# Moving the clamps of three weight blocks and the copies of five to GpSimd in a fused attention and feed-forward kernel

## The chip, the cores and the metric

The kernel runs on one core of a Trainium2 chip. Times are device microseconds of that core for one launch, from inputs in the chip's memory to the output in it. A profile is one execution of its own, with its own time; the times shown beside it are other executions.

## The reference

Three parts follow each other; the sizes are batch 4, 8 heads, 576 positions, head width 64, so 512 features.

```python
def _attn_ref(q, k, v):
    ...
    mask = (rel >= 0) & (rel < window)          # window 128
    scores = np.where(mask, scores + bias[None], -1000000000.0)
    attn = np.exp(scores - max)
    attn = attn / (np.sum(attn, axis=-1, keepdims=True) + 1e-09)
    return np.matmul(attn, v)

def _moe_ref(x, U, V, w_ch1, w_ch2):
    h = x.transpose(0, 2, 1) @ U @ V            # rank 32
    u = x + h.transpose(0, 2, 1)
    return u + np.maximum(u @ w_ch1, 0.0) @ w_ch2   # 2048 hidden

def _moe2_ref(x, w_in, w_spatial, b_spatial, w_out):
    h = np.maximum(x @ w_in, 0.0)
    u, v = h[..., :512], h[..., 512:]
    ...                                         # v normalised, mixed over positions
    return (u * v_s) @ w_out
```

The weights U, V, w_ch1, w_ch2, w_in and w_out arrive as 64-bit floats; the rest as 32-bit ones.

## The kernel before

**The work.** The kernel goes through the four batches of the attention, four pairs of heads each (`heads`, from L545). For a pair TensorE makes the scores (L577), VectorE adds the bias and finds the row's extreme (L589), ScalarE takes the exponentials with their sums (L594), and the rows are divided by their sums: L599 and L601 make the reciprocals on VectorE, then nine multiplies a pair follow, each either on GpSimd (L607) or on VectorE (L609). TensorE transposes the result (L616), ScalarE or VectorE copies it out of PSUM (L317, L318), and TensorE multiplies it with the values (L639). After the four pairs of a batch come the transposes of its output (L659) and the low-rank mix (L675, L687), whose result VectorE adds to `u` (L692).

The feed-forward part runs over groups of columns (positions of a batch). Its 2048 hidden units are cut into four parts of four blocks of 128. The **first part** is worked on while the attention still runs: five groups of 256 columns (`ffn_group` with `early`, called at L721) take TensorE's time wherever the attention leaves it, with the lowest priority. Such a group splits `u` into a high and a low half (L431 on ScalarE, L434 on GpSimd), multiplies with the first weights (L460 to L462), takes the positive part (L467, L469), multiplies with the second weights (L497 to L499) and adds (L507). Every float32 product is made as three products of rounded halves: high by high, low by high, high by low. The other columns and parts follow after the attention, then the last network.

**The weights of the first part.** They are eight blocks of 128 x 512, numbered c = 0 to 7: even numbers are the first weights of the four hidden blocks, odd ones the second weights (`part_of_hidden`, L388; called at L710). Each is made by `weights` (L373) in these steps:

- a DMA brings the 64-bit block (512 KB) into a buffer of the ring `wa` (L350);
- ScalarE takes the magnitude of the upper words into a buffer `st` (L356; the ring `st` has three buffers);
- VectorE clamps it to the range of exponents (L362), shifts it and masks it (L363), puts in the sign (L366) and the bits of the lower words (L369), all in place in `st`;
- ScalarE copies `st`, rounded, into the high half (L317, as a CAST that writes `wa`);
- GpSimd subtracts the high half from `st` and writes the low half (L384).

`single` (from L338) has the steps up to L369, and has two forms of the clamp: on VectorE, or on GpSimd if its last argument is true. `weights` has two forms of the high half: the copy on ScalarE, or a multiply by a broadcast 1.0 on GpSimd.

**What sets the order.** All operations are first listed as tasks with an engine (or several to choose from), a cost, what they read and write, and a priority. `Plan.run` (L169) then puts them in order with these costs: at each moment the engine that can begin first takes its ready task of the best priority, and each engine's instructions are written out in that order. It holds one more resource, `port`: a task of GpSimd and a VectorE task marked `port=True` (L362 to L369 and L609 among them) are never planned side by side. The planner's costs for 512 columns are 0.33 for a clamp on VectorE, 0.0034 x 512 + 0.15 = 1.89 for one on GpSimd, 0.52 for a copy on ScalarE and 0.0021 x 512 + 0.15 = 1.23 for an operation of two inputs on GpSimd. On the chip the order of each engine is fixed, and only the semaphore waits decide when an instruction begins. The DMAs are all issued by SyncE, in the planned order.

The constants stand in `K` (L956). `cp` and `wp` are read in one place alone, L712, where they say for each block c of the first part whether its clamp and its copy go to GpSimd:

```python
lambda c: (c < K["cp"], c < K["wp"])
```

Of the kernel before, what the change touches and what calls it, by code (L numbers as in the profile page):

```python
# [259 lines left out]
def tile_kernel(ctx, tc, qT, kT, v, U, V, w1, w2, w_in, wspT, bsp, w_out, bias, out):  # L260
# [32 lines left out]

    r_wa = Ring(in_left, "wa", max(12, 2 * K["parts"][0]))
    r_u = Ring(in_left, "u", 16)
    r_y = Ring(in_left, "y", 12)
    r_raw = Ring(in_left, "raw", 2)
    r_st = Ring(in_left, "st", K["nst"])
    r_h = Ring(in_left, "h", 8)
# [11 lines left out]

    PARTS = K["parts"]

# [10 lines left out]
    def engines(kind, usual):  # L324
        return BOTH if kind in K["flex"] else (usual,)

# [61 lines left out]
    def part_of_hidden(qi, ring, prio, early=lambda c: None, on_pool=lambda c: (False, False)):  # L388
        res = []
        for f in range(PARTS[qi]):  # L390
            c0 = (sum(PARTS[:qi]) + f) * 128
            two = []
            for i, args in enumerate(((block(w1, 0, E, c0, c0 + 128, 4), 4, 128), (block(w2, c0, c0 + 128, 0, E), 1, E))):
                c = 2 * f + i
                two.append(weights(ring, *args, prio(c), early(c), on_pool(c)))
            res.append(two)
        return res
# [142 lines left out]
    def low_rank_weights(prio, early, prio_v, early_v):  # L540
        single(u32, [(0, block(U, 0, 128, 0, RANK)), (1, block(U, 64, S, 0, RANK, 4))], 5, RANK, prio, None, early)
        P.add("DVE", 0.1, lambda: nc.vector.memset(u32[64:, 0], 0.0), w=[u32], prio=prio)
        single(v32, [(0, stacked(block(V, 0, RANK, 0, S), 4))], 1, S, prio_v, None, early_v)
# [152 lines left out]
    for pair in range(4):  # L696
        P.dma(128, 192, lambda pair=pair: nc.sync.dma_start(out=bias_t[:, pair], in_=bias[:, pair]),
              w=[bias_t.part(pair)], prio=20 * pair + 0.5)
    low_rank_weights(15, 2, 10 * K["low"], 10 * K["lowd"])
    parts_w = [None] * 4  # L700
    for b in range(B):
# [7 lines left out]
        if b == 0:  # L709
            parts_w[0] = part_of_hidden(0, r_wa, lambda c: 10 * (K["w0"] + K["w0s"] * c),  # L710
                                        lambda c: 10 * (K["d0"] + K["d0s"] * c),
# [241 lines left out]

K = dict(parts=(4, 4, 4, 4), flex='xeht', cp=0, wp=0, low=6, w0=8, w0s=1.23, nb=5, evac=40.0, nst=3, d0=7, d0s=0.91, lowd=5)  # L956


# [38 lines left out]
```

## Time and profile before

| | us |
|---|---|
| median of 3 runs | 779.35 |
| the three runs | 779.55, 779.35, 773.35 |
| the profiled execution | 775.38 |
| its span, first to last instruction | 773.6 |
| mean granted clock of TensorE, of full speed | 0.990 |

The span is the time from the first to the last instruction of the profiled execution; 1.8 us of its time lie around it. Engines are named in the rows as PE (TensorE's matmuls), PEld (its weight loads), DVE (VectorE), ACT (ScalarE), POOL (GpSimd) and SP (SyncE); L and a number is a line of the kernel. Start times are us from the start of the span.

### The profile page before, as it was taken

Reading aid. Unit: us, or ns where it says so; the run is one execution under the profiler, and the core shown is the slowest. Engines: PE = TensorE matmul, PEld = TensorE weight load, DVE = VectorE, ACT = ScalarE, POOL = GpSimd, SP = SyncE. Lnnn points to the kernel's source line nnn. Section 1 sums busy time; section 2 is a strip of 40 time slices with the busy share of each in tenths; the row PEclk is TensorE's granted clock in tenths of the full one; section 3 lists DMA queues with packets and bytes.
Section 4 is the critical chain, followed back from the end, with each engine's and each line's share of the span. In section 5 each row is a group of like instructions: output and inputs, shape, how many; then the busy total and the mean of one; then the engine's idle time right before and its main releaser. Section 6 shows DMA issues by size and latency. Waiting matters only on the chain.

```text
span 773.6 us, 13053 instructions
## 1 busy us (share of the span) xinstructions
PE 748.1 (97%) x4988; PEld 635.7 (82%) x4988; DVE 414.4 (54%) x1077; ACT 317.7 (41%) x856; POOL 263.7 (34%) x344
## 2 busy tenths in 40 slices
PE   6788999999899999999999999999999999999998
PEld 5566878889677888898888888888898898898987
DVE  5989677576699832237952272222845325325120
ACT  6767566574445422124531242321552332332322
POOL 1253231110655642125861253530555043043021
PEclk9989999999999999999999999999999999999999
DMA  7846213120605100024000110001300100200102
GB/s 216 278 153 187 63 42 114 35 76 1 219 15 175 43 1 1 1 83 134 1 1 0 60 51 1 0 1 50 105 1 1 55 1 1 69 1 1 55 1 68
DMA packets 28834, 45.70 MB, mean 59 GB/s; under 512 B 4964, under 2 KB 18020, under 8 KB 28772
## 3 DMA queue, kind: packets, MB, share of 16 engines
q1 hardware_dynamic: 28772, 44.87, 18.3%
q8 instruction: 39, 0.64, 0.3%
q14 instruction: 23, 0.19, 0.1%
HBM read 40.14 MB, written 4.72 MB: 58 GB/s over the span
## 4 chain that ended last, share of the span: by engine, by line
PE 87%; DVE 9%; ACT 2%; issue 1%; DMA 1%; SPq 0%; POOL 0%; ACTq 0%; DVEq 0%; POOLq 0%
PE sc L497 5%; PE sc L498 5%; PE sc L499 5%; PE at L460 5%; PE at L461 5%; PE at L462 5%; PE at L616 4%; PE at L639 3%; PE acc L497 3%; PE acc L499 3%; PE acc L498 3%; PE f L460 3%; PE at L780 3%; PE at L779 3%; PE at L781 3%; PE f L461 3%
## 5 line engine op out<-in xcount | busy, mean ns | idle before, releaser
L434 POOL TENSOR_TENSOR x<-u,xc 128x64 fp32r<-128x64 f32 (+5 forms) x108 | 92.8, 893 | 134.3 <-ACT xc L431 133.0
L469 DVE SCALAR_TENSOR_TENSOR h<-at,h 128x512 fp32r<-128x512 f32 (+1 forms) x51 | 32.7, 641 | 96.5 <-ACT h L467 96.5
L467 ACT ACTIVATE h<-at 128x512 fp32r<-128x512 f32 (+1 forms) x51 | 28.6, 560 | 125.9 <-PE at L462 125.8
L594 ACT ACTIVATE p<-p,nmax 128x192 f32<-128x192 f32 (+1 forms) x144 | 61.4, 430 | 9.4 <-DVE nmax L589 9.3
L616 PE MATMUL at<-ident,p 128*128 128x128 f32 x272 | 41.6, 296 | 6.2 <-DVE p L609 5.0
L589 DVE CUSTOM_DVE_ANT_0 p<-sc,bias 128x192 f32<-128x192 f32 (+1 forms) x144 | 39.8, 326 | 14.0 <-PE sc L577 13.9
L460 PE MATMUL at<-xc,wb 128*128 128x512 f32 (+1 forms) x120 | 44.2, 368 | 0.0
L497 PE MATMUL sc<-h,wb 128*128 128x512 f32 (+1 forms) x120 | 44.2, 368 | 0.0
L499 PE MATMUL sc<-h,wb 128*128 128x512 f32 (+1 forms) x120 | 44.1, 368 | 0.0
L498 PE MATMUL sc<-h,wb 128*128 128x512 f32 (+1 forms) x120 | 44.1, 368 | 0.0
L462 PE MATMUL at<-x,wb 128*128 128x512 f32 (+1 forms) x120 | 44.1, 368 | 0.0
L461 PE MATMUL at<-xc,wb 128*128 128x512 f32 (+1 forms) x120 | 44.1, 368 | 0.0
L577 PE MATMUL sc<-kr,qr 64*64 64x192 f32 (+2 forms) x576 | 33.5, 332 | 10.7 <-DMA kr<-in_kT 6.7
L616 PEld LDWEIGHTS at<-ident,p 128*128 128x128 f32 x272 | 33.0, 150 | 12.7 <-issue 4.2
L384 POOL TENSOR_TENSOR wa<-st,wa 128x512 fp32r<-128x512 f32 x24 | 32.6, 1367 | 31.4 <-ACT wa L317 27.8
L794 POOL TENSOR_TENSOR u<-y,u 128x576 fp32r<-128x576 f32 x16 | 23.1, 1459 | 55.6 <-ACT u L792 55.6
L384 POOL TENSOR_TENSOR wb<-st,wb 128x512 fp32r<-128x512 f32 x20 | 30.9, 1555 | 31.3 <-ACT wb L317 31.3
L469 DVE SCALAR_TENSOR_TENSOR h<-f,h 128x512 fp32r<-128x512 f32 (+1 forms) x27 | 17.8, 658 | 43.0 <-ACT h L467 42.9
L431 ACT CAST xc<-u 128x64 fp32r<-128x64 f32 (+5 forms) x108 | 38.3, 437 | 3.8 <-PE at L687 3.8
L467 ACT ACTIVATE h<-f 128x512 fp32r<-128x512 f32 (+1 forms) x27 | 15.4, 571 | 53.2 <-PE f L462 52.1
L497 PE MATMUL acc<-h,wa 128*128 128x256 f32 (+1 forms) x108 | 35.6, 329 | 1.5 <-DVE y L507 1.2
L577 PEld LDWEIGHTS sc<-kr,qr 64*64 64x64 f32 x576 | 21.8, 141 | 17.5 <-issue 10.1
(323 smaller groups left out, 2279.2 us busy)
## 6 DMA issues: line engine op xcount, KB each, us to landing
wa<-in_w SPq DMA_DIRECT2D x16, 512.0 KB, 4.9
wb<-in_w SPq DMA_DIRECT2D x16, 512.0 KB, 5.6
qr<-in_qT SPq DMA_DIRECT2D x16, 288.0 KB, 2.9
kr<-in_kT SPq DMA_DIRECT2D x16, 288.0 KB, 3.8
vr<-in_v SPq DMA_DIRECT2D x16, 256.0 KB, 2.8
wa<-in_w_in SPq DMA_DIRECT2D x8, 512.0 KB, 3.5
out<-h SPq DMA_DIRECT2D x15, 256.0 KB, 2.0
wb<-in_w_out SPq DMA_DIRECT2D x4, 512.0 KB, 4.0
```

Source lines behind the costliest of these rows:

```text
L384: P.add("POOL", pool_tt(k * c), lambda: nc.gpsimd.tensor_tensor(out=b[:, 1], in0=st.ap(), in1=f32(b[:, 0]), op=ALU.subtract), r=[st, b.par ...
L434: nc.gpsimd.tensor_tensor(out=tl[il][:, o : o + m], in0=ub[:, s : s + m], in1=f32(th[ih][:, o : o + m]), op=ALU.subtract)
L460: nc.tensor.matmul(o, wt[:, 0, k], a[ia], start=k == 0, stop=False)
L461: nc.tensor.matmul(o, wt[:, 1, k], a[ia], start=False, stop=False)
L462: nc.tensor.matmul(o, wt[:, 0, k], l[il], start=False, stop=k == 3)
L469: P.add("DVE", dve(per * n), lambda f1=f1, hh=hh, hl=hl: nc.vector.scalar_tensor_tensor(out=hl.ap(), in0=f1.ap(), scalar=0.0, in1=f32(hh.a ...
L497: nc.tensor.matmul(o, wt[:, 0, 0, c], hh[:, j], start=i == 0 and x == 0, stop=False, skip_group_check=True)
L498: nc.tensor.matmul(o, wt[:, 1, 0, c], hh[:, j], start=False, stop=False, skip_group_check=True)
L499: nc.tensor.matmul(o, wt[:, 0, 0, c], hl[:, j], start=False, stop=i == len(wts) - 1, skip_group_check=True)
L577: nc.tensor.matmul(s[o : o + 64, c0 : c0 + k1 - k0], qr[d, 64 * t : 64 * t + 64], kr[d, k0:k1], start=True, stop=True, skip_group_check=True)
L594: nc.scalar.activation(out=o(), in_=o(), func=AF.Exp, scale=-1.0, bias=nmax[:, sl, t : t + 1], accum_out=sums[:, sl, t : t + 1])
L616: P.add("PE", 0.109, lambda pt=pt, t=t, half=half, blk=blk: nc.tensor.transpose(pt[:, blk * 128 : blk * 128 + 128], p[:, t, half * 128 : h ...
```

## The change

Two constants change: `cp` from 0 to 3 and `wp` from 0 to 5. With that the clamp of the blocks c = 0, 1, 2 is an instruction of GpSimd instead of VectorE, and the high half of the blocks c = 0 to 4 is made by GpSimd's multiply by one instead of ScalarE's copy. The priorities and the DMAs' due times stay. The order is planned anew with the other engines and costs, so other instructions may change their places, and of the divisions of the softmax rows others may fall to GpSimd or VectorE.

```diff
-K = dict(parts=(4, 4, 4, 4), flex='xeht', cp=0, wp=0, low=6, w0=8, w0s=1.23, nb=5, evac=40.0, nst=3, d0=7, d0s=0.91, lowd=5)
+K = dict(parts=(4, 4, 4, 4), flex='xeht', cp=3, wp=5, low=6, w0=8, w0s=1.23, nb=5, evac=40.0, nst=3, d0=7, d0s=0.91, lowd=5)
```

What these constants choose between, in `single` and in `weights`:

```python
if pool:
    P.add("POOL", 0.0034 * n + 0.15, lambda: nc.gpsimd.tensor_scalar(out=st.ap(), in0=st.ap(), **cut), w=[st], prio=prio)
else:
    P.add("DVE", dve2(n), lambda: nc.vector.tensor_scalar(out=st.ap(), in0=st.ap(), **cut), w=[st], port=True, prio=prio)
...
if on_pool[1]:
    P.add("POOL", pool_tt(k * c), lambda: nc.gpsimd.tensor_tensor(
        out=b[:, 0], in0=st.ap(), in1=one[:, :1].rearrange("p (a b) -> p a b", a=1).broadcast_to([128, k, c]),
        op=ALU.mult), r=[st, one], w=[b.part(0)], prio=prio)
else:
    copy(engines("w", "ACT"), k * c, lambda: b[:, 0], st.ap, None, r=[st], w=[b.part(0)], prio=prio)
```

## Rows read from the trace of the kernel before

**Rows 1.** The page, part 1: busy time, share of span, instructions of each engine.
```profile
PE 748.1 (97%) x4988; PEld 635.7 (82%) x4988; DVE 414.4 (54%) x1077; ACT 317.7 (41%) x856; POOL 263.7 (34%) x344
```

**Rows 2.** Busy time by stretch; after the engines: granted clock, DMA share, GB/s.
```profile
28.00:78.00 50.00, 40.99 (x449) 32.34 (x450) 47.55 (x168) 37.55 (x124) 18.49 (x24) 0.90 0.62 194
20.00:40.00 20.00, 16.50 (x155) 12.41 (x157) 18.57 (x71) 15.04 (x51) 3.75 (x8) 0.88 0.87 285
40.00:60.00 20.00, 16.48 (x192) 12.35 (x192) 18.79 (x60) 14.37 (x47) 12.38 (x16) 0.86 0.43 133
60.00:80.00 20.00, 17.69 (x207) 14.36 (x208) 20.00 (x81) 15.95 (x55) 4.54 (x7) 1.00 0.60 176
80.00:200.00 120.00, 119.56 (x1349) 102.05 (x1348) 79.92 (x316) 67.54 (x236) 19.76 (x45) 1.00 0.18 53
200.00:220.00 20.00, 16.05 (x84) 13.36 (x83) 16.89 (x30) 10.65 (x22) 15.28 (x16) 1.00 0.63 225
34.00:36.00 2.00, 0.44 (x2) 0.47 (x3) 2.00 (x9) 1.41 (x3) 0.40 (x1) 0.80 0.75 205
36.00:38.00 2.00, 1.72 (x9) 1.32 (x8) 2.00 (x6) 1.07 (x2) 0.97 (x1) 0.50 0.96 311
```

Each row begins with the stretch and its length; then come the busy times (with instructions) of PE, PEld, DVE, ACT and POOL.

**Rows 3.** Timeline of TensorE: start, duration, instruction; in brackets the idle time before.
```profile
35.56 1.30 PE L616 MATMUL at<-ident,p 128*128 128x128 f32 x5 [2.57 <-DVE p L609]
...
52.03 0.41 PE L460 MATMUL f<-x,wa 128*128 128x256 f32 x1
...
66.86 1.70 PE L616 MATMUL at<-ident,p 128*128 128x128 f32 x13 [0.62 <-DVE p L609]
...
73.44 0.36 PE L460 MATMUL f<-x,wa 128*128 128x256 f32 x1
```

**Rows 4.** Groups by line of VectorE, 28 to 78: count, busy us, mean ns, idle.
```profile
L609 DVE TENSOR_SCALAR p<-p,rinv 128x192 f32<-128x192 f32 (+2 forms) x24 | 9.1, 444 | 0.0
L369 DVE SCALAR_TENSOR_TENSOR st<-wa,st 128x512 uint32<-128x512 uint32 x7 | 5.4, 777 | 0.0
L366 DVE SCALAR_TENSOR_TENSOR st<-wa,st 128x512 uint32<-128x512 uint32 x7 | 5.1, 729 | 0.0
...
L363 DVE TENSOR_SCALAR st<-st 128x512 uint32<-128x512 uint32 x8 | 3.9, 484 | 0.0
L362 DVE TENSOR_SCALAR st<-st 128x512 f32<-128x512 f32 x8 | 3.8, 473 | 0.0
```

**Rows 5.** Timeline of VectorE.
```profile
24.70 2.06 DVE L609 TENSOR_SCALAR p<-p,rinv 128x64 f32<-128x64 f32 x9
...
34.85 0.40 DVE L362 TENSOR_SCALAR st<-st 128x512 f32<-128x512 f32 x1
35.17 3.06 DVE L609 TENSOR_SCALAR p<-p,rinv 128x64 f32<-128x64 f32 x9
...
64.98 3.19 DVE L609 TENSOR_SCALAR p<-p,rinv 128x64 f32<-128x64 f32 x9
```

A row of several instructions in a run, as x9, names the shape of its first.

**Rows 6.** ScalarE: one group by line, 28 to 78, then two rows of its timeline.
```profile
L317 ACT CAST wa<-st 128x512 fp32r<-128x512 f32 x7 | 4.3, 615 | 2.4 <-DVE st L369 2.2
...
34.90 0.62 ACT L317 CAST wa<-st 128x512 fp32r<-128x512 f32 x1
36.69 0.48 ACT L317 COPY ph<-at 128x384 f32<-128x384 f32 x1 [1.17 <-PE at L616]
```

**Rows 7.** GpSimd: the subtraction to 100 us (ns least/median/most), the select from the groups.
```profile
L384 POOL TENSOR_TENSOR wa<-st,wa x8: 1262/1286/1371, 35.6 to 84.8; 128x512 fp32r<-128x512 f32 x8
...
masks.py:199 POOL TENSOR_SCALAR_AFFINE_SELECT ident<-ident 128x128 f32<-128x128 f32 x1 | 0.3, 292 | 0.0
```

**Rows 8.** Timeline of GpSimd.
```profile
35.60 1.37 POOL L384 TENSOR_TENSOR wa<-st,wa 128x512 fp32r<-128x512 f32 x1 [3.81 <-ACT wa L317]
...
57.16 1.69 POOL L607 TENSOR_TENSOR p<-p,rinv 128x64 f32<-128x64 f32 x4 [1.28 <-DVE nmax L589]
58.81 1.26 POOL L384 TENSOR_TENSOR wa<-st,wa 128x512 fp32r<-128x512 f32 x1
65.23 1.32 POOL L384 TENSOR_TENSOR wa<-st,wa 128x512 fp32r<-128x512 f32 x1 [5.16 <-ACT wa L317]
```

## The prediction

> **What bounds the kernel now.** I read the busy shares of the page first, to see which engine can set the end: TensorE is busy for 748.1 us of a span of 773.6, 97% [rows 1]. So nearly all of the time is matmul work that this change leaves alone, and what it can win or lose is TensorE's idle time. The second view is the table of stretches, which shows where that idle time lies [rows 2]: 3.50 us in 20 to 40, 3.52 in 40 to 60, 2.31 in 60 to 80, then 0.44 in the whole of 80 to 200, and 3.95 in 200 to 220. From 80 on TensorE has filler (hidden-layer groups of batches already done), so a delay that arises earlier finds no gap to be swallowed in and a gain found earlier is kept: either comes out at the end one for one. The edited steps run in 28 to 78. There TensorE is busy 40.99 of 50 us, VectorE 47.55, ScalarE 37.55, GpSimd 18.49: VectorE is the bound of the stretch, GpSimd has room. The third view, TensorE's own timeline, shows what VectorE's load does: transposes sat 2.57 us idle before 35.56 until L609 (the division of the softmax rows), and again 0.62 us before 66.86 [rows 3]. The grouped lines show what VectorE spends its 47.55 us on [rows 4]: L609 9.1, and the weight unpacking L362, L363, L366, L369 3.8, 3.9, 5.1 and 5.4.
>
> **Removed from VectorE: three clamps (L362).** The clamps are those of blocks 0, 1 and 2. One takes VectorE 0.32 us from its start to the next instruction's, as that of block 1, 34.85 to 35.17 [rows 5]; three are 1.0 us. Only that one stands plainly on the path, directly ahead of the nine L609 that TensorE waits 2.57 us for. The other two I can't place on it with a row, so I credit 0.32 in full and half of the other 0.66: **-0.65 us**.
>
> **Removed from ScalarE: five casts (L317).** Seven such casts take 4.3 us in the stretch, 0.615 each [rows 6], so five are 3.1 us. Behind that of block 0 (34.90) ScalarE sat idle 1.17 us before its next copy, waiting for transposes [rows 6]. Idle time of that kind hides the cast, and with 37.55 of 50 us busy ScalarE has it around the others too: **0 us**. If that cover were gone each would be worth 0.62 on a copy that TensorE waits for, 3.1 in all, which I keep as the end of the gain.
>
> **Added to GpSimd: five copies and three clamps.** The copy is a multiply of 128x512 by a broadcast one. Its nearest row is the subtraction of the same block, 128x512 on the same engine, 1.286 us median [rows 7]; five are 6.4 us. A clamp of 128x512 on GpSimd is nowhere in the trace. From below: the 128x128 select, one input, 0.292 us in all [rows 7], if its time doesn't grow with the columns (times four it is 1.17). From above: one such subtraction for each of the two operations in it, 2 x 1.286 = 2.57. I take 1.29, the row of the same shape, and keep 0.29 and 2.57 for the range: 3.9 us for three (0.9 to 7.7). GpSimd goes from 18.49 to 28.8 us of 50 (25.8 to 32.6): it doesn't become the bound by its own load.
>
> **The longer chain of a block.** A block's copy takes 1.29 instead of 0.62, so its parts are ready 0.7 us later, and a clamp of 1.29 in place of 0.41 adds 0.9 more. The matmuls of block 0 begin at 52.03 [rows 3], and its subtraction starts at 35.60 [rows 8]: 15 us of slack. Block 4's starts at 65.23 [rows 8] and is done by 66.6, its matmuls begin at 73.44 [rows 3]: 6.9 us. So 0.7 to 1.6 us later is hidden: **0 us**. If the plan tightens that slack, filler is missing where TensorE is idle, up to 1.6 us for a block. The x halves that GpSimd makes for the first group queue behind the weights in its stream; but the group is gated by VectorE's adds, and the plan gives the halves the higher priority, so I put nothing on it.
>
> **What the added GpSimd work costs VectorE.** This is the term that decides. Nine L609 with no arithmetic on GpSimd take 2.06 us (24.70); nine that meet one subtraction of GpSimd take 3.06 (35.17, beside 35.60) and 3.19 (64.98, beside 65.23) [rows 5, 8]. So one GpSimd operation of 1.3 us that meets SBUF work of VectorE costs VectorE 1.0 to 1.13 us. The Trainium skill, on its page SBUF — State Buffer (section SBUF: two separate sides), says that the two engines share a pair of ports under an exclusive lock, held for the whole instruction while the loser waits; the rows agree in size, and by the rule in full each meeting would cost the whole 1.29, 0.29 more than the lesser of my two rows; the forecast goes by the rows.
>
> How many of the eight new operations meet such work? Of the eight subtractions before 90 us, those of 35.60, 58.81 and 65.23 [rows 8] meet an L609 burst that TensorE then waits for: three of eight. Six of the new operations belong to blocks 0 to 2, before any filler exists: 6 x 3/8 x 1.0 = 2.25. Two fall later, where TensorE's waits behind such bursts are only some 0.6 us (the 66.86 row): 2 x 3/8 x 0.6 = 0.45. Together 2.7. The planner knows the port, will not start L609 while it counts GpSimd as busy and prices the clamp high, so it puts reads of PSUM beside the new work where it has some; I take a fifth off: **+2.15 us**. From the GPSIMD Engine Reference of the Trainium skill (Elementwise, side-by-side cycle accounting) an operation with one input runs at about 1.03 cycles an element at 1.2 GHz, an estimate of 0.44 us for the clamp; the three clamps would then meet less, and the sum fall by some 0.7 us. No run here shows it.
>
> **The sum.** -0.65 + 0 + 0 + 2.15 = **+1.5 us**. The profiled execution took 775.38 us, span 773.6 and 1.8 around it, so its own sum is 776.9. The three timed runs are 773.35, 779.35 and 779.55, median 779.35, 4.0 above the profiled one: the unchanged kernel scatters by 6.2 us. I start from the middle of the four executions, (775.38 + 779.35)/2 = 777.4, and predict **778.9 us**.
>
> **The rivals.** First, **the relief counts and the clock holds: faster.** In 34 to 36 TensorE is busy only 0.44 of 2 us, and its granted clock falls to 0.50 (the 1.2 GHz level) in 36 to 38 [rows 2]. If block 1's clamp no longer stands ahead of L609 and the new GpSimd work lands beside PSUM reads, the 2.57 us gap shrinks and the clock may stay at 2.4 GHz. If it stays low until the end of that burst's transposes and their products, 6 us of work at the lower level would be 3 at the higher. That gives 777.4 - 1.0 - 3.0 = 773.4. For it: GpSimd is busy only 18.49 of the 50 us. Against it: the gap would have to vanish almost entirely, and the clamp is 0.32 of 2.57.
>
> Second, **every meeting is paid: slower.** The copy of block 0 now comes directly behind L369 and ahead of its subtraction, in the place where the nine L609 of 35.17 become ready; copy, subtraction and the clamp of block 1 then hold three times 1.3 us there. If all eight operations meet a burst, that is 8 x 1.1 = 8.8 less the 0.32 of the clamp: 777.4 + 8.5 = 785.9. It decides from the point where more than four of the eight lie in bursts that TensorE waits for. For it: the SBUF work of VectorE (L609 and the four unpacking lines) is 27.3 us of the 50 [rows 4]. Against it: three of the present eight do. The lock told of in SBUF — State Buffer of the Trainium skill is the rule that speaks for this rival; by it the price would be 8 x 1.29, an end near 787.4.
>
> Third, **VectorE is given its work back: no change.** L607 and L609 are one division that the plan gives to GpSimd or VectorE, whichever is free. Four of them are on GpSimd at 57.16 [rows 8]; with GpSimd fuller they go to VectorE at 0.25 each, 1.0 us, and eat the three clamps, while meetings stay as many as now: 777.4.
>
> **How the numbers follow.** Forecast 778.9 (from 0 to 4 us above 777.4): 0.45. Faster, around 773.4: 0.27. No change, 777.4: 0.16. Slower, around 785.9: 0.12. A measurement of this kernel can tell about 1%, 7.8 us, from no change: below 771.6 lies only the far end of the first rival, 0.05; above 787.1 the far end of the second, 0.06 (clamps at 2.57 instead of 1.29 add up to 3.4 to it); within 1% 0.89. The range takes in the scatter of the unchanged runs and the first rival below, and the second above: 772 to 786. The forecast's own is 776 to 782.
>
> **What would show it.** Right: three L362 fewer on VectorE before 45 us and five casts fewer on ScalarE, GpSimd at 28 to 29 us in 28 to 78; L609 bursts near 35 us of 3 us or more with GpSimd's copy beside them; TensorE's idle time in 20 to 80 up from 9.3 to about 11 us, and 80 to 200 still full. Wrong: a clock of 1.00 through 34 to 42, a clamp on GpSimd far from 1.3 us, first hidden-layer matmuls later than 53 us because of a weight block, or the difference found after 200 us, where I put nothing.

## The result and the profile after

The changed kernel takes 781.88 us (median of 17 executions, 779.15 to 784.45), the kernel before, on the same chip, 776.73 (17 executions, 773.35 to 779.87). The ratio is 1.0065, with a 95% interval of 1.0048 to 1.0081: slower by 5.1 us (3.7 to 6.3), which is within the 1% that counts as no change. The forecast was 778.9, 1.5 us above its base of 777.4. The profiled execution after took 781.88, with a span of 780.1. One execution among all those timed for this document, 1869.48 us of copies_2_3_alone below, is left out of its kernel's figures as a slow one.

The page's busy shares of the kernel after, part 1:

```profile
PE 750.9 (96%) x4988; PEld 635.4 (81%) x4988; DVE 417.7 (54%) x1080; ACT 314.0 (40%) x848; POOL 273.8 (35%) x349
```

Against [rows 1], TensorE is busy 2.8 us longer with the same 4988 matmuls, and idle 29.2 us of the span instead of 25.5. The 6.5 us between the two profiled executions are thus 3.7 of idle time and 2.8 of matmuls that took longer. The stretches of the kernel after (columns as in [rows 2]) say where:

```profile
28.00:78.00 50.00, 39.89 (x418) 28.89 (x415) 43.19 (x145) 31.96 (x109) 24.26 (x27) 0.86 0.60 187
20.00:40.00 20.00, 15.62 (x153) 11.14 (x153) 19.71 (x71) 14.82 (x51) 9.51 (x12) 0.95 0.87 282
40.00:60.00 20.00, 15.49 (x183) 10.85 (x181) 15.86 (x55) 12.03 (x45) 12.63 (x17) 0.84 0.52 170
60.00:80.00 20.00, 18.14 (x186) 13.99 (x184) 17.43 (x68) 12.81 (x45) 6.37 (x10) 0.86 0.50 147
80.00:100.00 20.00, 17.65 (x199) 14.21 (x198) 15.79 (x43) 12.22 (x38) 6.65 (x11) 1.00 0.21 61
...
200.00:220.00 20.00, 16.14 (x139) 13.21 (x138) 13.12 (x26) 9.18 (x21) 12.98 (x14) 1.00 0.64 224
...
56.00:58.00 2.00, 0.27 (x7) 0.07 (x1) 1.28 (x9) 1.64 (x8) 1.58 (x4) 1.00 1.04 414
58.00:60.00 2.00, 1.97 (x15) 1.09 (x15) 2.00 (x10) 2.00 (x10) 2.00 (x4) 0.65 0.72 244
60.00:62.00 2.00, 1.78 (x8) 1.00 (x6) 2.00 (x3) 1.20 (x4) 2.00 (x3) 0.50 0.41 106
...
66.00:68.00 2.00, 2.00 (x16) 1.47 (x14) 1.91 (x10) 0.43 (x1) 0.00 (x1) 0.50 0.00 0
```

And 80 to 100 in the kernel before, which [rows 2] hold only as part of 80 to 200:

```profile
80.00:100.00 20.00, 19.81 (x221) 17.02 (x219) 12.44 (x35) 8.68 (x27) 3.58 (x9) 1.00 0.18 57
```

Idle time of TensorE grew by 0.88 us in 20 to 40 (4.38 against 3.50), by 0.99 in 40 to 60 and by 2.16 in 80 to 100, and shrank by 0.45 in 60 to 80. There the loss has its other form: the granted clock was 0.86 after and 1.00 before, and 186 matmuls were done where 207 were. Two-microsecond stretches show it at 0.50, the 1.2 GHz level, in 60 to 62 and again in 66 to 68. The first fall begins in 58 to 60, behind 56 to 58 where TensorE was busy 0.27 of 2 us; the wait there is for a division of GpSimd (57.93 below), and not yet for the long burst. The second comes behind 62 to 66, where TensorE was busy 2.36 of 4 us, in part waiting for that burst. The kernel before has one low stretch in this part, too, from 52 to 56, so the second fall is the one that it lacks. VectorE is no longer the full engine of 28 to 78: it is busy 43.19 us, not 47.55, and GpSimd 24.26, not the 28 to 29 that I expected to see.

Three timelines show what happened. First the divisions of the softmax rows on VectorE, after:

```profile
35.24 4.29 DVE L609 TENSOR_SCALAR p<-p,rinv 128x64 f32<-128x64 f32 x9
...
58.76 5.00 DVE L609 TENSOR_SCALAR p<-p,rinv 128x192 f32<-128x192 f32 x6
...
66.47 2.06 DVE L609 TENSOR_SCALAR p<-p,rinv 128x64 f32<-128x64 f32 x9
```

The same three bursts of the kernel before are those at 35.17 and 64.98 of [rows 5] and, between them, this one:

```profile
58.34 2.53 DVE L609 TENSOR_SCALAR p<-p,rinv 128x128 f32<-128x128 f32 x5
```

So the first burst went from 3.06 to 4.29 us, the second from 2.53 to 5.00 (with one division more), and the third back from 3.19 to the undisturbed 2.06. Beside the first two, GpSimd's timeline after:

```profile
34.93 2.00 POOL L360 TENSOR_SCALAR st<-st 128x512 f32<-128x512 f32 x1 [2.82 <-ACT st L356]
36.91 1.04 POOL L379 TENSOR_TENSOR wa<-st,one 128x512 fp32r<-128x512 f32 x1
38.02 1.39 POOL L384 TENSOR_TENSOR wa<-st,wa 128x512 fp32r<-128x512 f32 x1
...
57.58 1.12 POOL L607 TENSOR_TENSOR p<-p,rinv 128x64 f32<-128x64 f32 x3 [0.42 <-DVE nmax L589]
58.66 2.05 POOL L379 TENSOR_TENSOR wa<-st,one 128x512 fp32r<-128x512 f32 x2
60.67 2.52 POOL L384 TENSOR_TENSOR wa<-st,wa 128x512 fp32r<-128x512 f32 x2
```

At 58.66 the copies of blocks 2 and 3 begin, and because a copy is on the same engine as its subtraction now, both subtractions follow without a gap: 4.57 us of GpSimd beside six divisions. Before, one subtraction stood there (58.81 of [rows 8]), since the next had to wait for a cast of ScalarE. TensorE's timeline after, rows that answer to [rows 3], the one of 56.18 below from the kernel before:

```profile
35.73 1.81 PE L616 MATMUL at<-ident,p 128*128 128x128 f32 x11 [2.43 <-DVE p L609]
...
53.48 0.39 PE L460 MATMUL f<-x,wa 128*128 128x256 f32 x1
...
57.93 0.80 PE L616 MATMUL at<-ident,p 128*128 128x128 f32 x3 [1.73 <-POOL p L607]
...
63.37 1.00 PE L616 MATMUL at<-ident,p 128*128 128x128 f32 x7 [0.91 <-DVE p L609]
...
70.37 0.36 PE L460 MATMUL f<-x,wa 128*128 128x256 f32 x1
```

```profile
56.18 0.39 PE L460 MATMUL f<-x,wa 128*128 128x256 f32 x1
```

The transposes of the second burst come in pieces, and the last seven wait until 63.37. Groups of GpSimd by line after, 28 to 95, give the prices:

```profile
L360 POOL TENSOR_SCALAR st<-st 128x512 f32<-128x512 f32 x3 | 6.0, 2001 | 6.4 <-PE at L616 3.5 <-ACT st L356 2.8
L379 POOL TENSOR_TENSOR wa<-st,one 128x512 fp32r<-128x512 f32 x5 | 5.3, 1070 | 3.6 <-ACT st L356 2.6 <-DVE st L369 1.0
```

A clamp takes 2.00 us and a copy 1.07, 11.3 us for all eight.

### The profile page after: what moved, and what is told of

The parts are those of the page before. It is cut to its first block, busy times and chain, and to the rows that moved or that the text cites. A ratio compares the mean times of both kernels' runs of the same rounds, so it can differ in the third digit from the quotient of the medians.

```text
span 780.1 us, 13042 instructions
## 1 busy us (share of the span) xinstructions
PE 750.9 (96%) x4988; PEld 635.4 (81%) x4988; DVE 417.7 (54%) x1080; ACT 314.0 (40%) x848; POOL 273.8 (35%) x349
## 4 chain that ended last, share of the span: by engine, by line
PE 86%; DVE 8%; issue 2%; DMA 1%; ACT 1%; POOL 1%; SPq 1%; POOLq 0%; ACTq 0%; DVEq 0%
PE sc L498 5%; PE sc L497 5%; PE sc L499 5%; PE at L460 5%; PE at L461 5%; PE at L462 5%; PE at L639 4%; PE acc L497 3%; PE at L616 3%; PE acc L499 3%; PE f L460 3%; PE f L461 3%; PE acc L498 3%; PE f L462 3%; PE at L779 3%; PE at L781 3%
## 5 line engine op out<-in xcount | busy, mean ns | idle before, releaser
L589 DVE CUSTOM_DVE_ANT_0 p<-sc,bias 128x192 f32<-128x192 f32 (+1 forms) x144 | 40.4, 329 | 13.5 <-PE sc L577 13.5
L616 PEld LDWEIGHTS at<-ident,p 128*128 128x128 f32 x272 | 31.4, 146 | 17.1 <-DVE p L609 4.9
L384 POOL TENSOR_TENSOR wb<-st,wb 128x512 fp32r<-128x512 f32 x20 | 31.0, 1558 | 31.2 <-ACT wb L317 31.2
L384 POOL TENSOR_TENSOR wa<-st,wa 128x512 fp32r<-128x512 f32 x24 | 32.8, 1382 | 20.9 <-ACT wa L317 20.8
L609 DVE TENSOR_SCALAR p<-p,rinv 128x192 f32<-128x192 f32 (+2 forms) x121 | 37.1, 377 | 0.4
```

The costliest lines, as they stand in the source:

```text
L384: P.add("POOL", pool_tt(k * c), lambda: nc.gpsimd.tensor_tensor(out=b[:, 1], in0=st.ap(), in1=f32(b[:, 0]), op=ALU.subtract), r=[st, b.par ...
L616: P.add("PE", 0.109, lambda pt=pt, t=t, half=half, blk=blk: nc.tensor.transpose(pt[:, blk * 128 : blk * 128 + 128], p[:, t, half * 128 : h ...
```

## The experiments

The planner keeps GpSimd and VectorE out of each other's way: in its plan of the changed kernel the copies of blocks 2 and 3 begin after the second burst has ended. On the chip no semaphore makes GpSimd wait for that burst, and it ran them beside it. So two things could cost: the new order, or the new engines within it. Each kernel was timed in five rounds beside the kernel before on its chip; a time above before is worked out as (ratio - 1) x 776. A difference between two such times has an interval of its own, some 2 us either way here (taken from the intervals of the two ratios); differences that are not clear of it are marked.

**Order or engines.** In the first kernel the constants of before rule the planning, and the eight instructions are then issued on GpSimd in that order; the second does the opposite. In these two, and in all later kernels whose operations are moved one by one, the clamp stands on L360 and the cast on L379 whatever their engine.

```diff
-nc.vector.tensor_scalar(out=st.ap(), in0=st.ap(), **cut)
+(nc.gpsimd if issued else nc.vector).tensor_scalar(out=st.ap(), in0=st.ap(), **cut)
...
-lambda c: (c < K["cp"], c < K["wp"])
+lambda c: (c < K["cp"], c < K["wp"], c < 3, c < 5)      # planned (0, 0): old_order_new_engines
+lambda c: (c < K["cp"], c < K["wp"], c < 0, c < 0)      # planned (3, 5): new_order_old_engines
```

> The planner places everything as in the kernel before (TensorE's order is the same, instruction by instruction), and only at issue the three clamps and five high-half copies go to GpSimd. Order theory (the loss comes from the new order, in which weight blocks 2 to 4 are finished late and TensorE lacks filler): 0 to +2 us against before. Port theory (the loss comes from GpSimd's operations holding VectorE up in its L609 bursts, the forecast's term): +4 to +8 us, L609 bursts near 35 and 58 us of 4 us and more.

> The planner places everything as in the changed kernel (TensorE's order is the changed one), but the three clamps are issued on VectorE and the five copies on ScalarE. Order theory: +4 to +6 us against before, as in the changed kernel. Port theory: -1 to +1 us, with the L609 bursts near 35 and 58 us back to about 3 and 3.5 us.

The old order with the new engines came to 1.0022 [1.0002, 1.0042], 1.7 us above before; the new order with the old engines to 1.0007 [0.9987, 1.0027], 0.5 above. The order by itself costs nothing that can be measured; the new engines cost 4.5 us in the new order (1.0065 less 1.0007) and 1.7 us in the old. Neither theory came out whole: the port theory's 4 to 8 us for the old order missed, and so did the order theory's 4 to 6 us for the old engines. Most of the loss needs both the new order and the new engines. VectorE's bursts in old_order_new_engines:

```profile
36.17 4.57 DVE L609 TENSOR_SCALAR p<-p,rinv 128x64 f32<-128x64 f32 x9
...
59.54 3.09 DVE L609 TENSOR_SCALAR p<-p,rinv 128x128 f32<-128x128 f32 x5
...
67.17 3.05 DVE L609 TENSOR_SCALAR p<-p,rinv 128x64 f32<-128x64 f32 x9
```

They sum to 10.71 us, 1.9 more than in the kernel before (8.78), nearly all of it in the first. VectorE's bursts in new_order_old_engines:

```profile
36.84 2.05 DVE L609 TENSOR_SCALAR p<-p,rinv 128x64 f32<-128x64 f32 x9
...
58.69 1.46 DVE L609 TENSOR_SCALAR p<-p,rinv 128x192 f32<-128x192 f32 x6
...
64.60 2.06 DVE L609 TENSOR_SCALAR p<-p,rinv 128x64 f32<-128x64 f32 x9
```

All three are undisturbed, 5.57 us together, where before has 8.78 and after 11.35. It is no faster than before for that, so something else in the new order costs about as much as these shorter bursts save; what it is was not tried.

**Clamps or copies**, each with an order planned for it:

```diff
+K = dict(..., cp=3, wp=0, ...)     # clamps_only
+K = dict(..., cp=0, wp=5, ...)     # copies_only
```

> Clamps of blocks 0 to 2 on GpSimd, all copies on ScalarE, planned anew. If the clamps of 2.0 us each carry the loss: +3 to +5 us. If the copies carry it: -1 to +1 us.

> Copies of blocks 0 to 4 on GpSimd, all clamps on VectorE, planned anew. If the copies carry the loss (blocks 2 to 4 finish behind GpSimd's x halves): +3 to +6 us, with second f matmuls as late as 70 us. If the clamps carry it: -1 to +1 us.

The clamps alone came to 1.0013 [0.9988, 1.0038], the copies alone to 1.0077 [1.0048, 1.0106]. In copies_only, though, the first burst took 3.84 us and the second 2.05, and TensorE waited 3.09 us for VectorE's L589 ahead of 57.19: it loses in a place that the changed kernel doesn't have, and its order was not run with the old engines, so its 6.0 us say that a plan with the copies moved can cost, not that the copies do by themselves or where ours did.

**Which operations.** From here on the order is that of after, and only the engine of single operations changes: `c in (...)` for the clamps, then for the copies.

```diff
+lambda c: (c < K["cp"], c < K["wp"], c in (0, 1, 2), c in (0, 1, 4))   # copies_2_3_back
+lambda c: (c < K["cp"], c < K["wp"], c in (0, 2), c in (1, 4))         # both_bursts_free
+lambda c: (c < K["cp"], c < K["wp"], c in (), c in (2, 3))             # copies_2_3_alone
+lambda c: (c < K["cp"], c < K["wp"], c in (1,), c in (0,))             # first_burst_alone
+lambda c: (c < K["cp"], c < K["wp"], c in (0,), c in (1, 4))           # later_clamp_back
```

> The changed kernel's order; clamps of blocks 0 to 2 and copies of blocks 0, 1, 4 issued on GpSimd, copies of blocks 2 and 3 on ScalarE. Burst theory (the loss is the L609 bursts that GpSimd's new work stretches, 2.2 us at the one near 35 and 3.5 us at the one near 58): the second burst falls from 5.0 to 1.5 to 2.8 us, the first stays near 4.3, and the time is 2 to 3.5 us below the changed kernel's 781.88. Lateness theory (all five copies and three clamps each make their block late and starve TensorE): about two eighths of the loss, 1.3 us, is gained back, whatever the bursts do.

> The changed kernel's order; clamps of blocks 0 and 2 and copies of blocks 1 and 4 on GpSimd, the clamp of block 1 and the copies of blocks 0, 2, 3 on VectorE and ScalarE. Burst theory: both bursts near 2 us and the time at 776 to 778, as with all old engines, though four of the eight operations are on GpSimd. Lateness theory: half of the loss stays, 779 to 780.

> The changed kernel's order; only the copies of blocks 2 and 3 on GpSimd, all other copies and all clamps on ScalarE and VectorE. Port theory (GpSimd work that stands beside SBUF work of VectorE on TensorE's path is what costs): the burst near 58 goes from 1.5 back to 4 to 5 us and the time is 2.5 to 3.5 us above that of the same order with all old engines (776.72). Rival (the loss is spread over all eight operations): 1.1 us, two eighths of 4.5.

> The changed kernel's order; only the clamp of block 1 and the copy of block 0 on GpSimd. Port theory: the burst near 35 goes from 2.05 to about 4 us, and the time is 1 to 2 us above that of the same order with all old engines. Rival (spread over all eight): 1.1 us; this run alone can't tell them apart, the burst's length shows whether the mechanism is there.

> As both_bursts_free, and the clamp of block 2 back on VectorE too: clamp of block 0 and copies of blocks 1 and 4 on GpSimd. In both_bursts_free that clamp (43.24, 2.35 us) stood beside L362, L363 and L366 of VectorE just ahead of the adds L692 that open the next batch. Port theory: without it L363 x2 falls from 1.82 to about 0.8 us and the time to 776 to 778. Rival (what is left in both_bursts_free is another thing): no change, near 779.

With copies 2 and 3 back on ScalarE the kernel came to 1.0028 [1.0010, 1.0046]: 2.9 us (about 1.0 to 4.8) of the 5.1 gone. Alone, in a kernel that has nothing else of the change, the two copies cost 1.0049 [1.0027, 1.0070], 3.3 us (about 1.0 to 5.5) more than the same order without them. VectorE and GpSimd in copies_2_3_alone:

```profile
60.78 4.71 DVE L609 TENSOR_SCALAR p<-p,rinv 128x192 f32<-128x192 f32 x6
```

```profile
60.38 2.05 POOL L379 TENSOR_TENSOR wa<-st,one 128x512 fp32r<-128x512 f32 x2
62.40 2.52 POOL L384 TENSOR_TENSOR wa<-st,wa 128x512 fp32r<-128x512 f32 x2
```

The burst grew by 3.25 us (4.71 against 1.46) and the time by 3.3. So close an agreement is luck, given that interval; besides, the profiled execution is a long one (784.28 us, the median is 780.42), with its first burst at 39.87 against 36.84 in new_order_old_engines, before these copies begin.

The first burst is another matter. In first_burst_alone it took 4.19 us, 2.1 more than with the old engines, and the time was 1.0014 [0.9998, 1.0031], 0.5 us more, where I had expected 1 to 2: within the intervals, but no support for a price of one for one there. TensorE's rows show why it can be less. First new_order_old_engines, whose undisturbed burst begins at 36.84, then first_burst_alone, whose burst begins at 35.64:

```profile
37.24 3.61 PE L616 MATMUL at<-ident,p 128*128 128x128 f32 x17 [2.54 <-DVE p L609]
40.79 0.56 PE L639 MATMUL at<-ph,v 128*64 128x64 f32 x8
```

```profile
40.51 0.91 PE L639 MATMUL at<-ph,v 128*64 128x64 f32 x8
```

With the old engines the transposes of this burst took TensorE 3.61 us, longer than the 2.05 of the divisions, at a granted clock of 0.50 in 38 to 40; the products behind them (L639) began 3.95 us after the burst did. In first_burst_alone they began 4.87 us after it: a burst 2.1 us longer held TensorE up by 0.9. At the second burst the same distance went from 3.08 us (61.77 less 58.69) to 6.00 in copies_2_3_alone (66.78 less 60.78).

both_bursts_free was a plain miss: 1.0045 [1.0026, 1.0063], 3.5 us above before, with both bursts undisturbed (2.06 and 1.46 us). Its rows, GpSimd first, then VectorE:

```profile
43.24 2.35 POOL L360 TENSOR_SCALAR st<-st 128x512 f32<-128x512 f32 x1
45.57 1.03 POOL L379 TENSOR_TENSOR wa<-st,one 128x512 fp32r<-128x512 f32 x1
46.71 1.43 POOL L384 TENSOR_TENSOR wa<-st,wa 128x512 fp32r<-128x512 f32 x1
```

```profile
45.88 1.14 DVE L362 TENSOR_SCALAR st<-st 128x512 f32<-128x512 f32 x1
46.95 1.82 DVE L363 TENSOR_SCALAR st<-st 128x512 uint32<-128x512 uint32 x2
```

The clamp of block 2 has slipped to 43.24, with a copy and a subtraction behind it. The VectorE operations beside them are lengthened: the clamp on L362 to 1.14 us, where it takes 0.42 in the kernel after, and the pair on L363 to 1.82 from 0.76:

```profile
46.41 0.42 DVE L362 TENSOR_SCALAR st<-st 128x512 f32<-128x512 f32 x1
46.74 0.76 DVE L363 TENSOR_SCALAR st<-st 128x512 uint32<-128x512 uint32 x2
```

They are queued ahead of the adds of L692, which TensorE waits for. TensorE's row in both_bursts_free, then in later_clamp_back, where that clamp is taken back as well:

```profile
50.39 0.33 PE L577 MATMUL sc<-kr,qr 64*64 64x64 f32 x4 [1.79 <-DVE u L692]
```

```profile
49.87 0.33 PE L577 MATMUL sc<-kr,qr 64*64 64x64 f32 x4 [1.29 <-DVE u L692]
```

In new_order_old_engines that wait is 0.34 us. So a meeting outside the bursts can hold TensorE up too. The time of later_clamp_back was 1.0015 [0.9994, 1.0036], 2.3 us less, just clear of the interval; but only 0.5 us of the wait is gone, since another copy and subtraction still stand there, so how much of the 2.3 is the clamp's is not shown.

**Forcing the planned order in time.** A one-column clearing by VectorE of the half that GpSimd is about to write, put at the place that the plan gives to GpSimd's operation, makes GpSimd wait until VectorE has come that far.

```diff
+turn_ = lambda h: nc.vector.memset(f32(b[:, h, 0, :1]), 0.0) if c_ < 8 else None
...
-P.add("POOL", pool_tt(k * c), lambda: nc.gpsimd.tensor_tensor(
+P.add("POOL", pool_tt(k * c), lambda: (turn_(0), nc.gpsimd.tensor_tensor(
```

> The changed kernel with all its work on GpSimd; ahead of each copy and subtraction of the first part VectorE writes one column of the half that follows, at the place that the plan gives the GpSimd operation, so GpSimd can't run ahead of the plan into an L609 burst (13 memsets of one column added). Burst theory: the burst near 35 falls to about 3 us (the clamp of block 1 is still beside it), that near 58 to 1.5 to 2.8, and the time to 777.5 to 779.5. Lateness theory: waits only add to it, 782 to 785.

> The kernel before with the same waits ahead of its eight subtractions. Burst theory: its bursts near 35, 65 and 84 lose the 1.0 to 1.1 us that a subtraction takes from each, and the time is 1 to 3 us below before. Lateness theory: no gain, 0 to +2 us.

The changed kernel with 13 such waits came to 1.0027 [1.0014, 1.0039], nothing else altered: 2.9 us (about 1.3 to 4.5) less than without them. Its second burst took 1.46 us again. A wait makes no block ready earlier, so blocks made late do not explain this part of the loss; GpSimd and VectorE meeting in time does. The kernel before with eight was a miss: 1.0017 [0.9996, 1.0038] instead of a gain. Its bursts shrank to 2.05, 1.51 and 2.04 us, but TensorE now waited elsewhere for VectorE, in part for the clearings themselves:

```profile
44.20 1.29 PE L675 MATMUL at<-xt,u 128*32 128x128 f32 x36 [1.22 <-DVE wa L378]
...
46.72 0.84 PE L687 MATMUL sc<-v,th 32*128 32x288 f32 x1 [1.24 <-DVE th L318]
```

**Is it the port, or the blocks made later?** One more explanation fitted so far: blocks 2 and 3 made by another engine, and later. Three kernels put multiplies of a scratch tile, on which no data hang, at the places of copies 2 and 3 in new_order_old_engines (one, two or three at each); one lets the real copies wait past the burst, by a single clearing.

```diff
+(on_pool[2] and nc.gpsimd.tensor_tensor(out=scr.ap(), in0=scr.ap(), in1=one..., op=ALU.mult), nc.scalar.copy(...))
...
+(c_ == 2 and nc.vector.memset(f32(b[:, 0, 0, :1]), 0.0), nc.gpsimd.tensor_tensor(out=b[:, 0], ...))   # copies_2_3_wait
```

> The changed kernel's order with all old engines, and two multiplies of 128x512 added on GpSimd, on a buffer that nothing else uses, at the places of the copies of blocks 2 and 3. Nothing waits for them but what is behind them on GpSimd. Port theory: the burst near 58 goes from 1.5 to 3.5 us or more and the time is 1.5 to 3 us above the same order with old engines. Rival (the weights' lateness costs, not the sharing of ports): burst stays 1.5, time 776 to 777.5.

> Kernel: the order of after, every clamp on VectorE and every copy on ScalarE (as new_order_old_engines, 776.7 us), and four multiplies of a 128x512 scratch tile on GpSimd, two at each of the places where the copies of blocks 2 and 3 stood; nothing reads what they write. They are about 4 x 1.05 = 4.2 us of GpSimd work; in idle_work_at_second two of them ran at 53.97 to 56.13, so four should reach to about 58.3 and stand beside the six L609 near 55.4 and what follows them. Theory A (it is GpSimd's occupation of the port that makes the burst of 58 us long, whatever the instruction is for): the burst of six goes from 1.5 to 3 to 4.5 us, and the time is 1.5 to 3.5 us above new_order_old_engines, 778 to 780. Theory B (blocks 2 and 3 being made later, or by another engine, is what costs): the burst is lengthened or not, but the time stays within 1 us of new_order_old_engines, 776 to 777.7, since no data hang on these multiplies.

> Kernel: the order of after with all clamps and copies on the old engines, and six multiplies of a scratch tile on GpSimd (three at each place of copies 2 and 3), some 6.3 us on which no data hang. With four, GpSimd was busy from 58.0 to 65.5 and the burst of six took 3.4 us, the time 1.4 us above before. Theory A: the burst takes 4 to 5 us and the time is 2 to 5 us above before (779 to 782). Theory B: no more than 1.5 us above before, though the two subtractions behind also come 2 us later.

> Kernel: the order of after with nothing but copies 2 and 3 on GpSimd (copies_2_3_alone, 780.4 us), with the same single column cleared by VectorE ahead of copy 2. Theory A: the burst goes from 4.7 to 1.5 us and the time to 776.5 to 778, that of the same order with old engines (776.7) within a microsecond or so. Theory B: the time stays near 780.4.

The two multiplies of the first ran at 53.97 to 56.13, the burst at 55.39 took 2.00 us, short of the 3.5 or more that I expected, and the time was 0.9992 [0.9976, 1.0009]: they hardly met it, so it says little. Four of them gave a burst of 3.43 us and 1.0018 [0.9990, 1.0046], which holds both theories. Six gave 1.0037 [1.0021, 1.0053], 2.3 us (about 0.3 to 4.3) above the same order without them. VectorE and GpSimd in idle_work_thrice, whose burst stayed short of the 4 to 5 us that I expected:

```profile
55.83 3.58 DVE L609 TENSOR_SCALAR p<-p,rinv 128x192 f32<-128x192 f32 x6
```

```profile
54.42 7.01 POOL L379 TENSOR_TENSOR scr<-scr,one 128x512 f32<-128x512 f32 x6
61.39 2.70 POOL L384 TENSOR_TENSOR wa<-st,wa 128x512 fp32r<-128x512 f32 x2
```

And the two real copies, still on GpSimd but held back until VectorE is past the burst, cost nothing: copies_2_3_wait is at 0.9998 [0.9982, 1.0014], 4.0 us below copies_2_3_alone. Its rows:

```profile
54.55 1.47 DVE L609 TENSOR_SCALAR p<-p,rinv 128x192 f32<-128x192 f32 x6
...
56.24 0.06 DVE L379 MEMSET wa<- 128x1 f32 x1
```

```profile
56.40 2.04 POOL L379 TENSOR_TENSOR wa<-st,one 128x512 fp32r<-128x512 f32 x2 [2.12 <-DVE wa L379]
```

That settles it for these two copies: made on the new engine and up to 2.1 us later they are free. GpSimd work without any data on it is not; but in idle_work_thrice the two subtractions behind it end 8.3 us after the burst began, against 6.5 in copies_2_3_wait, so that kernel alone would not rule out that their lateness costs something.

**The whole change with the one wait.** Does that one clearing mend the changed kernel? And with the clamp of block 2 taken back too? The changed kernel was put beside the second once more, on the same chip.

```diff
+turn_ = lambda h: nc.vector.memset(f32(b[:, h, 0, :1]), 0.0) if (c_, h) == (2, 0) else None   # after_one_wait
...
+lambda c: (c < K["cp"], c < K["wp"], c in (0, 1), c in (0, 1, 2, 3, 4))                        # one_wait_clamp_2_back, with the same clearing
```

> Kernel: the changed kernel (781.9 us) with one instruction more: ahead of the copy of block 2, at that copy's place in the plan, VectorE clears one column of the half that the copy writes, so that GpSimd can't begin copies 2 and 3 before VectorE is past the six L609 there. Theory A (the loss comes from copies 2 and 3 meeting that burst): the burst near 58 us goes from 5.0 back to about 1.5 us, and the time falls by 2.5 to 5 us to 777 to 779.5. Theory B (blocks 2 and 3 made on GpSimd, and later, are the cost): the burst is short but the time stays at 781 to 783, since the blocks are made later still.

> Kernel: the changed kernel with the one cleared column ahead of copy 2 (after_one_wait, 1.0052 of before) and with the clamp of block 2 on VectorE again; the clamps of 0 and 1 and all five copies stay on GpSimd. Theory A (two places carry the loss: copies 2 and 3 at the second burst, and the clamp of block 2 beside the unpacking near 43 us): 1.000 to 1.002 of before, 0 to 1.5 us above it. Theory B (the loss is spread over all eight operations, or lies in the other order): 1.003 or more.

> Kernel: the changed kernel itself, on the same chip and beside the same runs of before as one_wait_clamp_2_back, so that the two can be subtracted. Theory A: 1.005 to 1.008 of before, that is 3 to 5 us above one_wait_clamp_2_back. Theory B: within 2 us of it.

after_beside repeats the loss: 1.0065 [1.0038, 1.0091]. after_one_wait came to 1.0052 [1.0034, 1.0071], though its second burst took 1.47 us: only 1.0 us came back by its ratio, where I had expected 2.5 to 5 (its median is 3.0 us below the changed kernel's, but on a chip where before is faster, too). With six executions the interval of that 1.0 reaches from about -0.9 to 2.9. one_wait_clamp_2_back came to 1.0036 [1.0016, 1.0055], not the 1.002 or less of theory A, and lies 2.3 us (about -0.2 to 4.8) below after_beside, between theory A's 3 to 5 and theory B's 2 or less. By these figures the two places do not carry the whole loss, though they are not far clear of the noise. What is left in that last kernel is a first burst of 4.48 us and a third of 2.77.

**All kernels with the order of after in one table.** Burst times are of the one profiled execution, the time above before is of the timed ones.

| kernel | three bursts, us | sum | above before, us |
|---|---|---|---|
| new_order_old_engines | 2.05, 1.46, 2.06 | 5.57 | 0.5 |
| later_clamp_back | 2.06, 1.47, 2.06 | 5.59 | 1.2 |
| both_bursts_free | 2.06, 1.46, 2.06 | 5.58 | 3.5 |
| idle_work_at_second | 2.05, 2.00, 2.05 | 6.10 | -0.6 |
| copies_2_3_wait | 2.05, 1.47, 2.77 | 6.29 | -0.2 |
| after_with_waits | 2.67, 1.46, 3.07 | 7.20 | 2.1 |
| idle_work_twice | 2.05, 3.43, 2.05 | 7.53 | 1.4 |
| first_burst_alone | 4.19, 1.46, 2.05 | 7.70 | 1.1 |
| copies_2_3_back | 4.47, 1.47, 2.05 | 7.99 | 2.2 |
| after_one_wait | 4.49, 1.47, 2.06 | 8.02 | 4.0 |
| idle_work_thrice | 2.05, 3.58, 2.77 | 8.40 | 2.9 |
| one_wait_clamp_2_back | 4.48, 1.46, 2.77 | 8.71 | 2.8 |
| copies_2_3_alone | 2.06, 4.71, 2.06 | 8.83 | 3.8 |
| the changed kernel | 4.29, 5.00, 2.06 | 11.35 | 5.0 |
| after_beside | 4.48, 5.00, 2.06 | 11.54 | 5.0 |

Without both_bursts_free, whose loss lies outside the bursts, a straight line through the other 14 rises by 0.86 us of time for each us of burst (correlation 0.89); with it, by 0.72 (0.77). The last two rows are the same kernel twice; without them and without both_bursts_free the slope is 1.0 (0.81). A single time has an interval of 1 to 2 us either way, so the order of neighbours in the table means nothing; the trend does. It holds for this order alone: by the line the kernel before, with 8.78 us of bursts, would stand at 3.0 and not at 0, and old_order_new_engines, with 10.71, at 4.6 and not at 1.7.

## Why the prediction was wrong

**What held.** The mechanism, and the place in part: VectorE's divisions are held up by GpSimd, TensorE's idle time in 20 to 80 rose from 9.3 to 10.8 us, and 100 to 200 stays full. But 80 to 100, which I had called full as well, does not: TensorE is idle 2.35 us there against 0.19, more than half of the 3.7 us of idle time. "From 80 on TensorE has filler" failed in that stretch. The last 20 us before 220, where I put nothing, are unchanged (16.14 against 16.05 in [rows 2]). That five casts off ScalarE are worth nothing is borne out as far as it was tried: no kernel was faster for it. The first hidden-layer matmuls came at 53.48, not held up by a weight block: the named sign for that, later than 53 because of a weight block, did not come: that group's block 0 was subtracted by 39.41. The measured 781.88 lies inside the stated 772 to 786, but that is no merit: the range was that wide for the scatter of three runs and for the rivals, and the base of 777.4 stood 0.7 us above the 776.73 of all 17 runs, which hid a part of the miss.

**The step that failed** is "What the added GpSimd work costs VectorE", put at +2.15 us. It measured 4.5 us in the order that the plan made for it (about 2.6 to 6.5). In the old order, whose rows the working was taken from, the same engines cost 1.7 us. Its working had three errors.

- The count. "Three of eight" was carried over from the present subtractions, as if the new operations were spread like them. They come in chains. Four of the eight (clamp 1, copy 0, copies 2 and 3) lie on a burst, and copies 2 and 3 pulled a second subtraction into theirs, since a subtraction no longer waits for ScalarE. In the old order the second burst grew only from 2.53 to 3.09 us. I had seen such a chain for block 0 only, and put it into a rival.
- The "fifth off" because "the planner knows the port". The plan keeps the two apart, but only in its own times; the program holds no wait for it. On the chip GpSimd ran the copies when their data were there, at 58.66, and the six divisions began at 58.76. One wait at that place made the copies free in copies_2_3_wait.
- The base. I counted the new meetings on top of the present ones. The new order by itself has none at these three bursts (5.57 us in place of 8.78); the new engines then add 5.78 us (11.35 less 5.57). At 0.86 for one that is 5.0, beside the 4.5 us measured between the two kernels of that order; but these two are among the points that gave the line, so this is no test of it. Against the kernel before the three bursts grew by 2.57 us only, near the 2.15 of the sum; that is luck, as the time grew by 5.1. That 5.57 instead of 8.78 gives no faster kernel contradicts "a gain found earlier is kept". In the profile of new_order_old_engines TensorE is idle 1.71 us in 80 to 100, where before has 0.19, as its filler comes later; that this is where the gain went was not tried.

The price of a meeting was near: I took 1.0 to 1.13 us for an operation of 1.3. In copies_2_3_alone 4.57 us of GpSimd lengthened the burst by 3.25, 0.71 of it; in [rows 5, 8] it was 0.73 and 0.86. The Trainium skill, SBUF — State Buffer (SBUF: two separate sides), has the engine that comes second fully blocked for the whole instruction of the other; the trace agrees in kind and falls short of the full 4.57.

**The prices of the operations.** The copy was taken as 1.29 and is 1.07; the clamp was taken as 1.29 and is 2.00, within its bounds of 0.29 and 2.57 but far from 1.3, which was one of the named signs of being wrong. The eight take 11.3 us and not 10.3. By the GPSIMD Engine Reference of the Trainium skill (Elementwise, side-by-side cycle accounting) the clamp was an estimated 0.44; the measured 2.00 decides, and it is far from it. GpSimd's 24.26 us in 28 to 78 are fewer than the forecast 28.8 because only four subtractions are left in that stretch, where before has seven (group L384, 5.2 us against 9.1): blocks have moved behind 78 in the new order.

**The clamps off VectorE, -0.65.** Not found. TensorE's wait ahead of the first transposes went from 2.57 to 2.43 us, 0.14 and not 0.32, and clamps_only is 1.0 us slower than before by its middle, with no change inside its interval; its first burst is lengthened to 4.05 us, so it does not measure the relief by itself.

**The longer chain, 0.** The warning in it came true in part: the second hidden-layer group began at 70.37, where in the timeline of before it began at 56.18. In copies_2_3_wait copies made later are free, so the 0 stands for a later copy. For the later filler it is open: new_order_old_engines has that order and costs only 0.5 us, but with 3.2 us less of bursts, and what uses that up was not found.

**The rivals.** "The clock holds" did not come: the mean granted clock in 28 to 78 went from 0.90 to 0.86, and in 60 to 80 from 1.00 to 0.86. "VectorE is given its work back" was small: three divisions on GpSimd at 57.58 instead of four, and in the whole run L607 goes from 26 to 23. "Every meeting is paid" set its point of decision at more than four of eight; exactly four met a burst, and the time came out between it (+8.5) and the forecast (+1.5).

**What stays open.** By their middles the parts do not add up to the whole. Copies 2 and 3 cost 3.3 us alone, and taking them back from the changed kernel gave 2.9, but keeping them there with the one wait gave only about 1.0; with intervals of some 2 us either way these three do not contradict each other. The first burst's 2.1 us cost about 0.5 alone. Where the rest of the loss, some 2 us, lies is not shown: the first burst, the clamp of block 2 and the later filler of the new order are candidates, and no kernel separated them. No version was clearly faster than before: copies_2_3_wait and idle_work_at_second are level with it.

## What to carry to other kernels

A planner that keeps two engines off a shared resource only in its own clock has not kept them apart on the chip: look for the semaphore that holds the one back, and if there is none, look at which instructions become ready together. Moving an operation to the engine that runs its successor removes a handover, and with it the pause in which another engine could use the port: price the whole chain that now runs in one piece, not the operation. Measure a move once with the order kept and the engines changed, and once the other way round; the two together tell the order's cost from the engines'.

## What the hardware showed that I had not expected

A clamp of 128x512 (two operations, one input) takes GpSimd 2.00 us, nearly twice the 1.04 to 1.07 of a multiply of the same block by a broadcast operand and more than the 1.28 of a subtraction with two full inputs; VectorE does that clamp in 0.42. And GpSimd's own operations varied where VectorE worked beside them: the subtraction took 1.26 to 1.39 us in most places and 1.75 in others (at 49.87 in copies_2_3_alone), and the clamp 2.35 at 43.24 in both_bursts_free; what lengthens them was not tried.
